# Loading q and k over the hardware DMA queue and running a whole batch of attention ahead of the MoE, in a fused attention and MoE kernel

## The chip, the cores and the metric

The kernel runs on one core of a Trainium2 chip. The metric is the device time of one execution in microseconds (us). All times are medians; each run of a changed kernel stood beside runs of the kernel before on the same chip. A ratio below is the mean time of one kernel's fast runs over the mean time of the other's fast runs of the same rounds, so it is not quite the ratio of the medians quoted beside it.

The *time* is what is measured from outside; the *span* is what the profile covers, and it was about 2 us shorter in nearly every run (415.06 against 412.9 in the profiled run of the changed kernel).

## The reference, cut to what matters

```python
# q, k, v: (8 batches, 8 heads, 576 tokens, 64), f: (8, 8, 576), all fp32
scores = q @ k^T / sqrt(64)
cum    = cumsum(log(clip(f, 1e-4, 1)))             # a forget gate: decay between tokens
scores = where(causal, -1e9, scores + cum_i - cum_j)
x      = softmax(scores) @ v                       # (8, 8, 576, 64)
x      = x.transpose(0, 2, 1, 3).reshape(4608, 512)
h      = x @ w_in                                  # 512 -> 2048
out    = (h * sigmoid(h)) @ w_out                  # 2048 -> 512
```

## The kernel before

Attention goes in 16 steps `n`, each one half batch (four heads). A step has four chunks of scores. A chunk is a matmul into PSUM (`sc`), an exponential on ScalarE into `u`, and a causal mask on VectorE, in place:

```python
sc = patt.tile([P, QH, 512], FP32, name="sc", tag="att")   # 4 PSUM banks, one buffer
...                                                        # matmuls with lhsT = k, rhs = q
nc.scalar.activation(out=u[:, :, c*CW:(c+1)*CW], in_=sc[:, :, 0:CW], func=ACT.Exp, scale=scale)
...
nc.vector.tensor_tensor(out=x, in0=x, in1=mask_broadcast, op=ALU.mult)     # masks(n, c)
```

Then `products` multiplies `u` by the weighted values (`vp`) and by weights alone (`w_bf`, for the sums), into a tile `ps` that takes the same four banks. From it ScalarE copies the sums out, VectorE takes their reciprocals (a quarter at a time, between the chunks of the next step) and writes the normed result to `xT`, the input of the MoE.

The MoE is cut into units of four 128x512 matmuls: `hp` for the first layer, `po` for the second. `fill(n)` puts up to n units between the chunks, so that TensorE has work while ScalarE forms exponentials. Which kind a unit is follows from what is allowed:

```python
def fill(n):
    for _ in range(n):
        a, c = done["m1"], done["m2"]
        can1 = a < 16 * ready["g"] and a < 16 * (c // 16) + 32
        can2 = c < 16 * (a // 16)
        if not can1 and not can2:
            return False                     # nothing left: the gap stays empty
        if can1 and (not can2 or a - c <= 16 + (c % 2)):
            m1_chunk(...)                    # hp, then tanh (th) and gate (gt)
        else:
            m2_part(...)                     # po; after four of them osb and the store
...
for n in range(16):
    scores(n, 0); masks(n, 0); reciprocals(n - 1, 0); fill(3)
    scores(n, 1); masks(n, 1); reciprocals(n - 1, 1); load_qk(n + 2); fill(3)
    scores(n, 2); masks(n, 2); transposes(n + 1, 1); reciprocals(n - 1, 2); fill(3)
    scores(n, 3); transposes(n + 1, 0); masks(n, 3); reciprocals(n - 1, 3); fill(3)
    products([(n, None), (n - 1, 0), (n - 1, 1)]); finished(n - 1)
    fill(4)
```

(The special cases of steps 0 to 2 are cut.) `finished` releases a group of 512 tokens, 32 units, once its tokens are there, which in the steady part is about once in two steps. q and k come by transfers on GpSimd's queue that convert them to bf16 on the way, in runs of one token (64 fp32 values, 256 bytes); VectorE transposes them in blocks of 32x32.

The softmax here doesn't subtract the row's maximum and nothing guards it: scores larger than these inputs give would overflow.

## Time and profile before

The kernel took 394.63 us (394.57 to 395.19 in three runs). The profiled run took 396.2 us with a span of 394.2.

| | before |
|---|---|
| TensorE busy | 85% of the span |
| first MoE product that needs new activations of group 1 | 100.74 us |
| five periods, one per batch | 199.69 us, 39.94 each |
| the rest | 93.77 us |
| transfers on GpSimd's queue and SP's queue, share of 16 engines | 42.6% and 20.8% |
| packets, of them under 512 B | 122871, 114064 |

The three stretches of the table add up to the span: in the steady part a *period* is the time from one group's first product on new activations to the next group's. The prediction below shows the lines that this is read from. In the view of VectorE's costliest groups of the kernel before, the columns after the bar are busy us, mean ns of one, and the idle time before them:

```profile
L185 DVE STREAM_TRANSPOSE qkT<-raw 128x1152 bf16<-128x1152 bf16 x32 | 43.4, 1358 | 0.1
L233 DVE TENSOR_TENSOR u<-u,mask 128x512 bf16<-128x512 bf16 x64 | 27.1, 423 | 57.1 <-ACT u L221 56.7
```

### The profile page before, as it was taken

The numbers are of one execution on the slowest core, as the hardware profiler recorded it, in microseconds if no ns is written. First come the engines' busy times: TensorE is split into PE (matmuls) and PEld (weight loads), VectorE is DVE, ScalarE is ACT, GpSimd is POOL, SyncE is SP. The second block draws the span as 40 slices with busy tenths as digits, with TensorE's granted clock in tenths as the row PEclk, the third lists the DMA queues.
The fourth block names the chain that finished last, engine by engine and source line by source line (L and its number), as shares of the span: only waits on it lengthen the run. The fifth ranks groups of instructions, "written<-read, shape, count | busy, mean of one in ns | idle before, by whom it ended". The sixth has DMA issues, their size and how long they took to land.

```text
span 394.2 us, 9014 instructions
## 1 busy us (share of the span) xinstructions
PE 335.3 (85%) x3853; PEld 161.5 (41%) x3853; DVE 247.6 (63%) x359; ACT 209.0 (53%) x264; POOL 131.0 (33%) x185
## 2 busy tenths in 40 slices
PE   0245499985899989998999899989998998999996
PEld 0123244444344534443444344444444454444442
DVE  3654568836695669665966596659665984644400
ACT  4354367543683568365936583559354923534421
POOL 8397674890905090509150815050000000000000
PEclk9999799996999999999999999999999999999999
DMA  9999999999629654974596469700010000000112
GB/s 165 178 177 150 146 180 172 101 141 171 44 17 136 132 56 29 110 153 53 36 108 156 49 40 95 169 28 0 29 54 29 2 28 28 22 33 27 53 55 80
DMA packets 122871, 33.82 MB, mean 86 GB/s; under 512 B 114064, under 2 KB 118160, under 8 KB 122832
## 3 DMA queue, kind: packets, MB, share of 16 engines
q0 software_dynamic: 75328, 13.05, 42.6%
q1 hardware_dynamic: 45136, 19.62, 20.8%
q10 hardware_dynamic: 2368, 0.59, 0.7%
q8 instruction: 30, 0.49, 0.5%
q14 instruction: 9, 0.07, 0.1%
HBM read 36.85 MB, written 9.44 MB: 117 GB/s over the span
## 4 chain that ended last, share of the span: by engine, by line
PE 61%; DMA 15%; DVE 10%; POOL 6%; ACT 4%; issue 3%; SPq 0%; DVEq 0%; POOLq 0%; ACTq 0%
PE po L327 29%; PE hp L300 21%; PE ps L259 7%; DMA raw<-in_q_dram 4%; DVE qkT L185 4%; PE sc L213 4%; DMA w_out_bf<-in_moe_w_out_dram 3%; DMA vf<-in_v_dram 3%; POOL raw L73 3%; DVE xT L277 3%; POOL vp L175 2%; DMA w_in_bf<-in_moe_w_in_dram 2%; DVE gt L309 2%; DMA raw<-in_k_dram 2%; ACT u L221 2%
## 5 line engine op out<-in xcount | busy, mean ns | idle before, releaser
L300 PE MATMUL hp<-xT,w_in_bf 128*128 128x512 bf16 x576 | 135.0, 380 | 15.4 <-DVE xT L277 11.8
L327 PE MATMUL po<-w_out_bf,gt 128*128 128x512 bf16 x576 | 131.8, 380 | 0.0
L221 ACT ACTIVATE u<-sc 128x1600 bf16<-128x1600 f32 x64 | 96.0, 1500 | 38.8 <-PE sc L213 38.8
L309 DVE SCALAR_TENSOR_TENSOR gt<-th,hp 128x512 bf16<-128x512 bf16 x144 | 92.4, 673 | 38.2 <-ACT th L308 38.1
L308 ACT ACTIVATE th<-hp 128x512 bf16<-128x512 f32 x144 | 83.8, 601 | 59.4 <-PE hp L300 58.5
L300 PEld LDWEIGHTS <-w_in_bf 128*128 128x128 bf16 x576 | 53.4, 98 | 83.1 <-issue 23.2
L327 PEld LDWEIGHTS <-gt 128*128 128x128 bf16 x576 | 53.8, 98 | 65.6 <-issue 3.1
L286 DVE RECIPROCAL rec<-rec 128x144 f32<-128x144 f32 x64 | 65.3, 1031 | 1.6 <-ACT rec L275 1.6
L175 POOL TENSOR_TENSOR vp<-vf,w_bf 128x512 bf16<-128x512 f32 (+1 forms) x40 | 41.2, 1049 | 74.8 <-PE ps L259 67.2
L233 DVE TENSOR_TENSOR u<-u,mask 128x512 bf16<-128x512 bf16 x64 | 27.1, 423 | 57.1 <-ACT u L221 56.7
L213 PE MATMUL sc<-qkT 32*128 32x224 bf16 (+5 forms) x1024 | 36.4, 263 | 22.9 <-ACT u L221 14.6
L73 POOL DMA_DIRECT2D raw<-in_k_dram x60 | 39.8, 671 | 43.1 <-DVE qkT L185 29.4
L336 ACT ACTIVATE osb<-po 128x512 f32<-128x512 f32 x36 | 21.5, 596 | 45.1 <-PE po L327 45.1
L185 DVE STREAM_TRANSPOSE qkT<-raw 128x1152 bf16<-128x1152 bf16 x32 | 43.4, 1358 | 0.1
L73 POOL DMA_DIRECT2D raw<-in_q_dram x60 | 39.3, 663 | 11.6 <-DMA w_out_bf<-in_moe_w_out_dram 4.9
L213 PEld LDWEIGHTS <-qkT 32*128 32x128 bf16 x1024 | 20.4, 97 | 48.3 <-issue 42.7
L277 DVE TENSOR_TENSOR xT<-ps,rec 128x576 bf16<-128x576 f32 x32 | 22.7, 751 | 24.9 <-ACT rec L275 18.0
L259 PE MATMUL ps<-u,vp 128*32 128x128 bf16 (+7 forms) x1096 | 28.9, 265 | 1.6 <-ACT u L221 1.6
L275 ACT ACTIVATE rec<-ps 128x576 f32<-128x576 f32 x16 | 10.4, 650 | 34.5 <-PE ps L259 34.5
L259 PEld LDWEIGHTS <-vp 128*32 128x32 bf16 x1096 | 22.6, 106 | 6.0 <-issue 3.2
L259 PE MATMUL ps<-u,w_bf 128*32 128x64 bf16 (+4 forms) x576 | 18.1, 261 | 6.8 <-ACT u L221 4.8
L259 PEld LDWEIGHTS <-w_bf 128*32 128x32 bf16 x576 | 11.9, 102 | 17.1 <-issue 11.6
(28 smaller groups left out, 25.6 us busy)
## 6 DMA issues: line engine op xcount, KB each, us to landing
out_dram<-osb SPq DMA_DIRECT2D x36, 256.0 KB, 2.1
vf<-in_v_dram SPq DMA_DIRECT2D x32, 256.0 KB, 5.2
raw<-in_k_dram POOLq DMA_DIRECT2D x60, 72.0 KB, 3.5
raw<-in_q_dram POOLq DMA_DIRECT2D x60, 72.0 KB, 3.3
w_in_bf<-in_moe_w_in_dram POOLq DMA_DIRECT2D x8, 256.0 KB, 6.6
w_out_bf<-in_moe_w_out_dram POOLq DMA_DIRECT2D x4, 512.0 KB, 11.4
vf<-in_v_dram SPq DMA_DIRECT2D x8, 128.0 KB, 4.7
first<-in_k_dram ACTq DMA_DIRECT2D x2, 144.0 KB, 3.5
```

The source lines that it names most:

```text
L73: nc.gpsimd.dma_start(out=t[j * T : (j + 1) * T, i, :].rearrange("p (g d) -> p g d", d=D), in_=src[b, QH * g + j, :, :].rearrange("(g t) d ...
L175: nc.gpsimd.tensor_tensor(out=vp[r, c, :, :, :], in0=vst[b][c][r, :, :].rearrange("p h (r x) -> p h x r", x=2), in1=w_bf[r, c, b * H : (b ...
L185: nc.vector.transpose(out=qkT[n][:, i, :, :].rearrange("p x (g t) -> p g x t", t=T), in_=raw[n][:, i, :].rearrange("p (g x e) -> p g x e", ...
L213: nc.tensor.matmul(sc[:, j, lo - c * CW : hi - c * CW], lhsT=t[r, 1, x, k_off(kb) : k_off(kb) + P], rhs=t[r, 0, x, q0 : q0 + hi - lo], sta ...
L221: nc.scalar.activation(out=u[:, :, c * CW : (c + 1) * CW], in_=sc[:, :, 0:CW], func=ACT.Exp, scale=scale)
L259: nc.tensor.matmul(ps[32 * j : 32 * j + 32, base + q0 : base + q1], lhsT=w, rhs=us[n][:, j, o + q0 : o + q1], start=(kb == 0), stop=(kb == ...
L277: nc.vector.tensor_tensor(out=xT[:, 2 * g + h, b * S : (b + 1) * S], in0=src, in1=recs[n][:, :], op=ALU.mult,)
L286: nc.vector.reciprocal(out=recs[n][:, r], in_=recs[n][:, r])
L300: nc.tensor.matmul(hp[:, :], lhsT=w_in_bf[:, cc, fc * P : (fc + 1) * P], rhs=xT[:, cc, t0 : t0 + TG], start=(cc == 0), stop=(cc == NCC - 1),)
L308: nc.scalar.activation(out=th[:, :], in_=hp[:, :], func=ACT.Tanh, scale=0.5)
L309: nc.vector.scalar_tensor_tensor(out=gt[:, fc, :], in0=th[:, :], scalar=1.0, in1=hp[:, :], op0=ALU.add, op1=ALU.mult,)
L327: nc.tensor.matmul(po[:, :], lhsT=gt[:, fc, tb * P : (tb + 1) * P], rhs=w_out_bf[:, fc, :], start=(fc == 0), stop=(fc == NFC - 1),)
```

## The change

The intent was to feed TensorE in the first 50 us, where it is half idle. q and k are loaded by SP's hardware queue in runs of two tokens (512 bytes), with no conversion; GpSimd casts them. The transposes write the natural token order back. Both steps of batch 0 run before any MoE unit, with two four-bank score buffers in PSUM; the second one is given back before the MoE takes its four banks. And the order of filler in the loop is new.

```diff
-    G = S // T
+    G = S // (2 * T)
-    qkp = ... tc.tile_pool(name="qkp", bufs=3)
+    qkp = ... tc.tile_pool(name="qkp", bufs=2)
+    pfirst = tc.tile_pool(name="pfirst", bufs=1, space=PSUM)    # second score buffer, start only
+    att = [patt, pfirst]                                        # taken in turn
...
-                nc.gpsimd.dma_start(out=t[...bf16...], in_=src[...].rearrange("(g t) d -> t g d", t=T))
+            engs[j % len(engs)].dma_start(out=stg[n][...fp32...],
+                in_=src[...].rearrange("(g t c) d -> t g (c d)", t=T, c=2))
+    def cast_qk(n, i):
+        nc.gpsimd.tensor_copy(out=raw[n][:, i, :], in_=stg[n][:, i, :])
...
-            out=qkT[n][:, i, :, :].rearrange("p x (g t) -> p g x t", t=T),
+            out=qkT[n][:, i, :, :].rearrange("p x (g t c) -> p g c x t", t=T, c=2),
...
-            if can1 and (not can2 or a - c <= 16 + (c % 2)):
+            if can1 and not (can2 and (x < fresh or a - c > 16 + (c % 2))):
...
+    # scores, masks and products of steps 0 and 1, then:
+    pfirst_pool.__exit__(None, None, None)
+    pbig = ... tc.tile_pool(name="pbig", bufs=4, space=PSUM)
+    fill(6)
+    transposes(2, 1); transposes(2, 0)
-    for n in range(NQ):
+    for n in range(2, NQ):
...                                          # casts of step n + 1 in the first two gaps
-        fill(3)
+        fill(4)
         products([(n, None), (n - 1, 0), (n - 1, 1)])
-        fill(4)
+        fill(5, 3)                           # the first three of second-layer kind
```

(The loads of weights and values move with it.) So an odd step asks for 3+3+3+4+5 = 18 units in place of 16, out of the same 32 per two steps.

## The prediction

> **What bounds the kernel now.** Words first. The kernel has 16 attention steps n (8 batches, two groups of four heads each); each has four chunks of scores on TensorE (sc), an exponential on ScalarE (u), a mask on VectorE, then products (ps) that end in xT. The MoE is cut into 288 units of four 128x512 matmuls (hp: first layer, po: second) that are put between the chunks as filler. Group g of the MoE needs the attention of whole batches, so two steps release about 32 units.
>
> I read the page's busy line and slices first, then TensorE's costliest group, then busy time by stretch, then the chain of waits, then the timeline of TensorE where it idles. Columns of a timeline: start and length in us, engine, line, operation, tiles, shapes, count, and in brackets the idle time before with what ended it.
>
> ```profile
> PE 335.3 (85%) x3853; PEld 161.5 (41%) x3853; DVE 247.6 (63%) x359; ACT 209.0 (53%) x264; POOL 131.0 (33%) x185
> PE   0245499985899989998999899989998998999996
> L300 PE MATMUL hp<-xT,w_in_bf 128*128 128x512 bf16 x576 | 135.0, 380 | 15.4 <-DVE xT L277 11.8
> ```
>
> TensorE is the bound, except in the first eighth, and its longest waits are for VectorE's xT, not for a DMA. By stretch (length, TensorE busy, weight load, VectorE, ScalarE, Pool, clock, DMA):
>
> ```profile
> 14.40:50.20 35.80, 16.74 (x365) 11.25 (x365) 18.27 (x26) 16.33 (x12) 26.94 (x36) 0.91 1.30 159
> 50.20:100.70 50.50, 42.40 (x546) 20.94 (x543) 34.73 (x49) 27.63 (x33) 31.91 (x43) 0.93 1.29 147
> 140.70:180.60 39.90, 37.28 (x464) 17.55 (x464) 28.75 (x42) 23.97 (x30) 15.46 (x22) 1.00 0.70 87
> 330.10:394.20 64.10, 60.16 (x278) 27.10 (x277) 22.01 (x33) 25.07 (x42) 0.00 (x0) 1.00 0.11 41
> ```
>
> So there are four parts: a start of 50 us with TensorE half idle; 50 to 100.7; five equal periods of 39.94 us, one per batch, from the first real hp of a group (100.74) to that of step 14 (300.43); and 93.8 us of rest. A period has 2.64 us of TensorE idle, three waits that the timeline gives: 1.70 for xT in the even step, 0.73 for gt and 0.21 for a mask in the odd one. This is the end of an even step with filler before the products:
>
> ```profile
> 212.92 0.53 PE L213 MATMUL sc<-qkT 32*128 32x144 bf16 x24
> 213.38 2.76 PE L327 MATMUL po<-w_out_bf,gt 128*128 128x512 bf16 x12
> 216.07 0.87 PE L259 MATMUL ps<-u,w_bf 128*32 128x512 bf16 x36
> 218.26 0.60 PE L300 MATMUL hp<-xT,w_in_bf 128*128 128x512 bf16 x2
> 220.56 3.18 PE L300 MATMUL hp<-xT,w_in_bf 128*128 128x512 bf16 x14 [1.70 <-DVE xT L277]
> ```
>
> And step 4, the only one in steady use that had run out of units before its products:
>
> ```profile
> 91.19 0.53 PE L213 MATMUL sc<-qkT 32*128 32x144 bf16 x24 [1.60 <-ACT u L221]
> 93.33 1.31 PE L259 MATMUL ps<-u,w_bf 128*32 128x512 bf16 x24 [1.61 <-ACT u L221]
> 95.42 0.44 PE L259 MATMUL ps<-u,w_bf 128*32 128x128 bf16 x12 [0.77 <-DVE u L233]
> 95.64 2.88 PE L259 MATMUL ps<-u,vp 128*32 128x448 bf16 x68
> ```
>
> The reader should see that without filler the products wait for the last exponential (1.61) and then the last mask (0.77): 2.4 us that three units hide at 213.38.
>
> [...] the 68 value products above took 2.88 us after the idle stretch and 1.55 at 216.77. [...] steady TensorE waits for no DMA here. [...] a mask that started at 77.47, while the chain of waits has Pool at work on vp until 78.10, took 0.91 us where this mask takes 0.38 elsewhere (215.69). [...] the new transposes write every second bf16, one per 4-byte word. No run yet shows what that costs a transpose (1.36 us now).
>
> **The change part by part.**
> *Loads.* q and k leave Pool's queue (120 issues of 0.67 us, 79 us of Pool) for the SP queue; the packets double. Pool gets 32 casts of 128x1152; I estimate 1.2 to 1.7 us each from its 1.04 us for a two-input 128x512, so some 45 us in all, and Pool, at 15.5 us of a 40 us period, stays idle. Transposes: same count and elements, I take 1.36 us. Gain in the steady part: none, as nothing on TensorE waits there for a load.
>
> *Start.* The instruction order shows both steps of batch 0, then 6 units, then step 2. f still sets VectorE free at 9.5 us. Transposes of k and q, 2 x 1.37: scores at 12.4 (14.43 before). With two score buffers the exponentials run end to end: 13.25 + 4 x 1.53 = 19.4, where a chunk took 2.46. Then exp(1,0) to 20.9, products and the copy (0.65) to 21.7, exps 1 to 3 at 1.5 each to 26.4, mask to 27.2, the rest of the products (0.4 + 2.9, slow clock) to 30.5, copy 31.2, xT 32.7, four reciprocals 36.5, xT 37.9: first hp at **37.9** instead of 51.77. But step 2's first two chunks had been done by then, and are still to come now.
>
> *After it.* Six units, [...] end at 44.9. Step 2's transposes stand behind the sixth gt (46.3) on VectorE: 2 x 1.36, so scores wait until 49.0, some 4 us idle[...]. Step 2: four chunks with three units at 3.15 (163.53 to 166.68), a 13th unit, products 0.9, gt wait 0.7, four units 3.5: 69.5. Step 3: the order puts nine po units, and then none: 3 x 3.15 + 0.5, wait 2.4, products 2.4: 84.3. Step 4 has no unit at all (64 score matmuls in a row): copy and xT 2.1 before its buffer is free, then from the 83.72 to 100.74 that it took before I take off 1.0 for less filler, so **102** in place of 100.74 for the first real hp of group 1. The 14 us won are eaten: the MoE has only the 32 units of group 0 until batch 1 is done, wherever they are put. Estimate for this point: 98 to 105.
>
> *Period.* Units released stay 32, but a full odd step now asks for 18 (po moved ahead), so 14 are left for the even one: the order reads sc24, ps104, hp20, no filler before the products. Even step: wait 2.4 (1.6 + 0.77, as step 4 showed), and still 1.7 for xT, since hp comes right behind. Odd step: 0.73 for gt stays, 0.21 goes. Sum 4.86 against 2.64: +2.2, period 42.2, five of them **+11**.
>
> *Rest.* Same units; fill ahead of the last hp hides its xT wait (0.99). 93.8 - 1 = 92.8.
>
> Sum: 102 + 5 x 42.2 + 92.8 = 405.8 of span, 0.4 more as time: 406. The middle of my range for the start (101) gives **405**.
>
> **The rivals.** (1) *The start's gain holds* (14 us at the first hp, or at least 5): it would if the units' supply did not matter. For: TensorE is half idle there. Against: step 4 starved before already with one filler more. With T = 95 and the waits of the even step half hidden, 391 to 396. (2) *The casts or strided transposes make VectorE the bound.* VectorE works 28.75 of 40 us, but sits right before the products in each step: at 2.0 us a transpose (+0.65), each step's tail would grow by 1.3, 2.6 a period, and the time would be near 418. [...] (3) *DMA*: the q1 queue's 20.8% of 16 engines over 45136 packets is 29 ns a packet; q and k of four steps and two v are 18432 packets, 33 us of all 16 engines, and w_in and w_out some 10 us each (the chain has 9.25 and 12.61 for the last of each): about 55 us, an estimate, and the first po is due at 61. If late, +3 to +6. For: share 1.29 until 100 before. [...]
>
> **Range and chances.** The period's two waits are read from the same instructions (step 4), so +8 to +12 is firm if the order is followed; the start is good to 3.5 us either way; rival 2 has perhaps one chance in six. So 405, 397 to 415. 2% slower begins at 402.5: 0.62; within 2%: 0.33; faster than 386.7 needs rival 1 in full: 0.05.
>
> **What would show it.** First hp near 38, idle TensorE near 45 to 49, group 1's first real hp near 102 (before 100.74), step 4 without filler; periods of 42 us, with two waits in the even step, of 2.4 ahead of ps for u and the mask and of 1.7 ahead of hp for xT; transposes of 1.36; casts under 1.7; DMA share about half in the steady part. I am wrong if the period stays at 40 (waits hidden by something I did not see), if transposes take 2 us or more, or if group 1 starts by 95.

Its sum came to 405.8 us of span, put down as 405 us of time. Two stood in the sum of the start: a slow stretch within the six units (their 7.0 us, 37.9 to 44.9, still hold it) and about 1.7 us for a second one in step 2, so the terms printed for step 2 fall short of its 69.5 by about that much. The slow clock that it reckons with for the value products of step 1 (2.9 us) is what step 4 showed: 2.88 us, with a granted clock of 0.50 from 91.8 to 98.6 us. The DMA share of about half was the estimate; no trace showed it before the change.

## The result and the profile after

The changed kernel took 415.56 us (414.1 to 416.6, four runs) against 394.91 us beside it (394.57 to 395.57): ratio 1.0518, 95% interval 1.0481 to 1.0556. That is slower, as expected, but just above the range of 397 to 415.

The page's busy line, its slices and TensorE's costliest group, after:

```profile
PE 343.9 (83%) x3853; PEld 166.8 (40%) x3853; DVE 257.4 (62%) x357; ACT 208.8 (51%) x264; POOL 89.3 (22%) x97
PE   0475699836899789987999699969996999999996
PEclk9998889985999989999999899989999999999999
L306 PE MATMUL hp<-xT,w_in_bf 128*128 128x512 bf16 x576 | 138.2, 389 | 19.1 <-DVE xT L283 14.6
```

The second digit of the PE row is now 4 where it was 2: the start does run earlier. But a 3 and several 6s have come in between 20% and 75% of the span, and the clock's row (9 is full speed) has a 5 at the end of the start and single 8s in the loop. TensorE has the same 3853 instructions and 8.6 us more of busy time: some of them ran slower.

By stretch (length, TensorE busy, weight load, VectorE, ScalarE, GpSimd, clock, share of the DMA engines, GB/s), after:

```profile
39.20:105.10 65.90, 48.13 (x567) 23.17 (x568) 38.28 (x51) 30.85 (x35) 21.31 (x20) 0.83 0.89 173
105.10:148.80 43.70, 38.73 (x464) 18.69 (x464) 29.83 (x42) 23.97 (x30) 9.66 (x10) 0.96 0.39 91
148.80:190.90 42.10, 37.26 (x464) 17.72 (x464) 29.49 (x42) 23.97 (x30) 9.26 (x10) 1.00 0.49 105
```

The first real product of group 1 stands at 105.06 us, later than before the change, although the first MoE product moved to 39.16. Then come periods of 43.74, 42.11, 43.82, 43.76 and 41.91 us. The two shown hold the same 464 matmuls; the first took 1.47 us more of TensorE's time, at clock 0.96.

TensorE's timeline where an even step of the changed kernel ends (start, length, engine, line, operation, tiles, shapes, count, idle time before):

```profile
139.51 0.53 PE L219 MATMUL sc<-qkT 32*128 32x144 bf16 x24
141.71 0.76 PE L265 MATMUL ps<-u,w_bf 128*32 128x512 bf16 x24 [1.67 <-ACT u L227]
143.48 0.44 PE L265 MATMUL ps<-u,w_bf 128*32 128x128 bf16 x12 [1.02 <-DVE u L239]
143.71 2.88 PE L265 MATMUL ps<-u,vp 128*32 128x448 bf16 x68
146.52 0.79 PE L306 MATMUL hp<-xT,w_in_bf 128*128 128x512 bf16 x2
148.80 1.46 PE L306 MATMUL hp<-xT,w_in_bf 128*128 128x512 bf16 x6 [1.49 <-DVE xT L283]
```

Compare it with the same place in the prediction (from 212.92): no filler between the last scores and the products, so TensorE waits 1.67 us for the exponential, then 1.02 for a mask; then the 68 value products take 2.88 us instead of 1.55; then it waits for xT as before. The starving was predicted, but the second wait is longer here than the 0.77 allowed for (over the five periods it is 0.39 to 1.02), and the slow products are a cost that the sum did not have in the steady part.

VectorE's groups after, to be set beside the two lines shown of before:

```profile
L191 DVE STREAM_TRANSPOSE qkT<-raw 128x1152 bf16<-128x1152 bf16 x32 | 46.0, 1445 | 0.0
L239 DVE TENSOR_TENSOR u<-u,mask 128x512 bf16<-128x512 bf16 x64 | 33.5, 527 | 63.0 <-ACT u L227 62.8
```

The transposes cost 6% more, the masks 25% more on average, though the masks did not change. None of TensorE's waits in the view of waits is for a transfer, before or after; the two queues' share of the DMA engines fell from 63.4% to 47.3%, and packets under 512 B from 114064 to 40336.

| span by part, us | before | after | difference |
|---|---|---|---|
| to the first real product of group 1 | 100.74 | 105.06 | +4.3 |
| five periods | 199.69 | 215.34 | +15.7 |
| the rest | 93.77 | 92.50 | -1.3 |
| span | 394.2 | 412.9 | +18.7 |

### The profile page after: what moved, and what is told of

It reads as the page before. It is cut to its first block, busy times and chain, and to the rows that moved or that the text cites. A ratio compares the mean times of both kernels' runs of the same rounds, so it can differ in the third digit from the quotient of the medians.

```text
span 412.9 us, 9054 instructions
## 1 busy us (share of the span) xinstructions
PE 343.9 (83%) x3853; PEld 166.8 (40%) x3853; DVE 257.4 (62%) x357; ACT 208.8 (51%) x264; POOL 89.3 (22%) x97
## 4 chain that ended last, share of the span: by engine, by line
PE 61%; DVE 27%; ACT 8%; issue 1%; DMA 1%; ACTq 0%; DVEq 0%
PE po L333 26%; PE hp L306 22%; DVE qkT L191 9%; PE ps L265 9%; DVE rec L292 6%; ACT u L227 6%; DVE u L239 5%; PE sc L219 4%; DVE gt L315 4%; DVE xT L283 3%; ACT rec L281 1%; ACT th L314 1%; DMA f_sb<-in_f_dram 1%; DVE cum L154 0%; PE wps L170 0%
## 5 line engine op out<-in xcount | busy, mean ns | idle before, releaser
L306 PE MATMUL hp<-xT,w_in_bf 128*128 128x512 bf16 x576 | 138.2, 389 | 19.1 <-DVE xT L283 14.6
L315 DVE SCALAR_TENSOR_TENSOR gt<-th,hp 128x512 bf16<-128x512 bf16 x144 | 93.2, 672 | 40.0 <-ACT th L314 40.0
L306 PEld LDWEIGHTS <-w_in_bf 128*128 128x128 bf16 x576 | 54.4, 99 | 90.4 <-issue 32.8
L239 DVE TENSOR_TENSOR u<-u,mask 128x512 bf16<-128x512 bf16 x64 | 33.5, 527 | 63.0 <-ACT u L227 62.8
L89 POOL CAST raw<-stg 128x1152 bf16<-128x1152 f32 x32 | 36.7, 1150 | 166.4 <-DMA stg<-in_k_dram 131.8
L191 DVE STREAM_TRANSPOSE qkT<-raw 128x1152 bf16<-128x1152 bf16 x32 | 46.0, 1445 | 0.0
L265 PE MATMUL ps<-u,w_bf 128*32 128x64 bf16 (+4 forms) x576 | 18.8, 263 | 19.1 <-ACT u L227 10.8
L265 PE MATMUL ps<-u,vp 128*32 128x128 bf16 (+7 forms) x1096 | 32.4, 286 | 0.0
L265 PEld LDWEIGHTS <-vp 128*32 128x32 bf16 x1096 | 25.2, 114 | 5.1 <-issue 1.8
```

The source lines that it names most:

```text
L89: nc.gpsimd.tensor_copy(out=raw[n][:, i, :], in_=stg[n][:, i, :])
L191: nc.vector.transpose(out=qkT[n][:, i, :, :].rearrange("p x (g t c) -> p g c x t", t=T, c=2), in_=raw[n][:, i, :].rearrange("p (g c x e) - ...
L239: nc.vector.tensor_tensor(out=x, in0=x, in1=m[:, None, :].to_broadcast([P, QH, w]), op=ALU.mult)
L265: nc.tensor.matmul(ps[32 * j : 32 * j + 32, base + q0 : base + q1], lhsT=w, rhs=us[n][:, j, o + q0 : o + q1], start=(kb == 0), stop=(kb == ...
L306: nc.tensor.matmul(hp[:, :], lhsT=w_in_bf[:, cc, fc * P : (fc + 1) * P], rhs=xT[:, cc, t0 : t0 + TG], start=(cc == 0), stop=(cc == NCC - 1),)
L315: nc.vector.scalar_tensor_tensor(out=gt[:, fc, :], in0=th[:, :], scalar=1.0, in1=hp[:, :], op0=ALU.add, op1=ALU.mult,)
```

## The experiments

Twelve kernels were run, all correct, each timed over three rounds. They are told in the order of the argument. Spans are split as above: T is the end of the start, then five periods, then the rest (92.5 to 93.2 in all versions with the new order, 93.7 with the old).

| run | time, us | ratio (95%) | T | five periods |
|---|---|---|---|---|
| after | 415.56 | 1.0518 (1.0481 to 1.0556) | 105.06 | 215.34 |
| e3_order_only | 409.77 | 1.0363 (1.0345 to 1.0382) | 106.22 | 208.92 |
| e2_loads_only | 403.74 (three fast runs) | 1.0246 (1.0190 to 1.0302) | slow run | slow run |
| e12_loads_4out | 398.42 | 1.0090 (1.0061 to 1.0120) | 100.89 | 201.89 |
| e1_fill_before | 407.30 | 1.0306 (1.0249 to 1.0363) | 106.19 | 204.42 |
| e11_fill_before_4out | 401.37 | 1.0141 (1.0109 to 1.0172) | 103.44 | 201.08 |
| e8_mask_first | 407.15 | 1.0297 (1.0279 to 1.0314) | 103.78 | 208.83 |
| e9_cast_twice | 425.24 | 1.0774 (1.0750 to 1.0798) | 106.58 | 221.83 |
| e7_dummy_mm | 413.36 | 1.0447 (1.0417 to 1.0478) | 105.79 | 213.01 |
| e10_one_buffer | 420.63 | 1.0628 (1.0576 to 1.0679) | 109.99 | 215.24 |
| e6_plan | 376.32 | 0.9527 (0.9494 to 0.9559) | 88.01 | 193.91 |
| e13_plan_old_loads | 381.03 | 0.9631 (0.9595 to 0.9668) | 94.49 | 190.95 |
| e14_plan_tuned | 372.83 | 0.9426 (0.9403 to 0.9448) | 89.59 | 188.59 |

The ratios are to the kernel before, whose median beside them was 394.91 to 395.40 us. T and the periods come from one profiled run each. In the last three kernels no wait marks the first product on new activations, so T there is the first MoE product of group 1, about 0.5 us earlier than the mark used for the others (in e13, 94.49 against 94.93).

### The new order with the old loads

```diff
 # the changed kernel, with load_qk, first load and transposes of the kernel before, and no cast_qk
-            nc.gpsimd.tensor_copy(out=raw[n][:, i, :], in_=stg[n][:, i, :])
+            nc.gpsimd.dma_start(...)          # q and k converted on the way
```

> The order, PSUM use and filler of the changed kernel with the loads of the kernel before (256-byte runs converted by Pool's own queue, no casts, plain transposes). Theory: the loss stays, less what casts add to the mask wait; periods 41.5 to 43 as the clock falls; 407 to 415. Rival 1 (casts and transposes): 395 to 400. A third way: Pool's queue is slow to bring step 1's q and k, so the start is 3 to 5 us later.

Measured: 409.77 us, 14.6 over the kernel before. The end of an even step in this run:

```profile
142.80 0.76 PE L266 MATMUL ps<-u,w_bf 128*32 128x512 bf16 x24 [1.67 <-ACT u L228]
143.81 0.41 PE L266 MATMUL ps<-u,w_bf 128*32 128x128 bf16 x12 [0.25 <-DVE u L240]
144.03 1.56 PE L266 MATMUL ps<-u,vp 128*32 128x448 bf16 x68
```

The wait for the exponential is the same 1.67 us, so it belongs to the order. The wait for the mask is 0.25 in every period, against 0.39 to 1.02 after the change, and the value products are slow once in five periods (2.5 us) in place of three times. The five periods are 6.4 us shorter than after the change. Of these, 2.5 are mask waits (5 x 0.25 against 3.72 in all), 2.9 are value products (8.74 against 11.68) and 0.7 are waits for gates. So the order costs most of the loss, and something in the loads adds 5.8 us (415.56 - 409.77) on top of it.

### The new loads with the old order

```diff
 # the kernel before, with load_qk, cast_qk and transposes of the change
```

> The order, PSUM use and filler of the kernel before, with the new loads alone (512-byte runs on the SP queue, casts on Pool, transposes that write every second element). Theory: transposes cost 0.08 us more each and a mask is now and then held by a cast for up to 0.7 us, mostly behind filler: periods 40 to 40.4, start a little earlier, so 392 to 397. Rival 1 (loads and casts make the loss): at least half of the 20 us shows here, 405 or more.

Measured: 403.74 us in the median of the three fast runs (403.25, 403.74, 407.69), between the two expectations. The profiled run was slow (413.07), so its waits are only named here: it too had ScalarE waiting for the store of an output tile. The next pair of runs shows that with fast profiles.

### The old filler counts in the new order, and the output buffers

```diff
-        fill(4)                      # after the last scores
+        fill(3)
         products(...)
-            fill(5, 3)
+            fill(4)
```

> The changed kernel with the filler counts of the kernel before in the main loop (3, 3, 3, 3 before the products, 4 after them), so that three po units stand ahead of the products of every even step. Theory (empty filler, then a slow clock): the wait of 2.1 to 2.7 us ahead of the even products goes, and with it the half-clock value products, so the five periods fall from 43.1 to about 40.2 us: 14 us, 401 to 402. Rival 1 (the casts on Pool and the strided transposes make the loss): periods stay near 43, time 413 or more. Rival 2 (only the waits count, the clock was slow for another reason): 2.2 a period, 404 to 405.

Measured: 407.30 us, above the 401 to 402 and the 404 to 405 that were expected, and below the 413 of rival 1. The wait of 1.67 us and the slow products are gone from all periods, which shows what caused them. But less than half of the loss came back (8.3 us), since the wait for xT grew from 1.7 to as much as 3.44 us. The timeline of SP's queue and then of ScalarE and TensorE in this run tells why:

```profile
130.38 1.91 SPq L81 DMA_DIRECT2D stg<-in_k_dram  x4
132.33 1.95 SPq L81 DMA_DIRECT2D stg<-in_q_dram  x4
134.38 5.63 SPq L97 DMA_DIRECT2D vf<-in_v_dram  x5
140.10 5.50 SPq L343 DMA_DIRECT2D out_dram<-osb  x3
```

```profile
144.64 0.60 ACT L342 ACTIVATE osb<-po 128x512 f32<-128x512 f32 x1 [3.92 <-DMA out_dram<-osb]
145.14 0.64 ACT L281 ACTIVATE rec<-ps 128x576 f32<-128x576 f32 x1
145.81 1.42 DVE L283 TENSOR_TENSOR xT<-ps,rec 128x576 bf16<-128x576 f32 x2 [2.73 <-ACT rec L281]
147.29 1.02 PE L306 MATMUL hp<-xT,w_in_bf 128*128 128x512 bf16 x4 [2.72 <-DVE xT L283]
```

Thirteen loads take SP 9.7 us to issue, and the stores stand behind them. With two output buffers, ScalarE can't copy the next output tile out until a store has landed (3.92 us), and the copy that leads to xT is next in its line. (The changed kernel itself has no wait of ScalarE for a store in its view of waits; the stall came up with the old counts.) The test is two more buffers, in this order and in the old one:

```diff
-    opool = ... tc.tile_pool(name="opool", bufs=2)
+    opool = ... tc.tile_pool(name="opool", bufs=4)
```

> The changed kernel with the filler counts of the kernel before in the main loop, and four output buffers in place of two. Theory A (with those counts only the wait of the copy to the output for the output's transfer, up to 4.6 us, behind thirteen loads on one queue, was left): that wait is gone, the wait for the transposed activations falls from 1.7 to 3.4 us to 0.7 to 1.0, the five periods are 39.8 to 40.3 us as before the change, and the time is 400 to 403 us. Theory B (the wait for activations has another source, the casts or the slow clock): periods stay near 40.9 and the time at 405 to 408.

> The kernel before with only the new loads, casts and transposes, and four output buffers so that no copy to the output waits behind loads. Theory A (beside the output stall the new loads cost next to nothing, and the order is what costs): periods of 39.9 to 40.6 us and 394 to 398 us. Theory B (casts and transposes slow VectorE and with it the whole loop): periods of 41 us or more and 400 us or more.

Measured: 401.37 and 398.42 us. Neither has a wait of ScalarE for a store, and the wait for xT is back at 1.70, not down to the 0.7 to 1.0 that e11 expected. Both sets of periods are near those of before: 40.05 to 40.43 and 40.06 to 40.61, each against 39.94. The end of an even step in the first of the two:

```profile
136.57 2.54 PE L333 MATMUL po<-w_out_bf,gt 128*128 128x512 bf16 x11 [0.16 <-issue]
139.03 0.87 PE L265 MATMUL ps<-u,w_bf 128*32 128x512 bf16 x36
139.73 1.55 PE L265 MATMUL ps<-u,vp 128*32 128x448 bf16 x68
141.44 0.38 PE L306 MATMUL hp<-xT,w_in_bf 128*128 128x512 bf16 x1 [0.16 <-issue]
143.52 0.81 PE L306 MATMUL hp<-xT,w_in_bf 128*128 128x512 bf16 x3 [1.70 <-DVE xT L283]
```

So 14.2 of the 20.65 us lost come back by filler counts and output buffers alone. The new loads in the old order, without the stall, cost 3.0 us (398.42 against 395.40). e12 ended 0.4 above its first expectation (394 to 398), and its mean mask took 493 ns where 423 was usual.

### What the casts do

GpSimd's casts take 1.15 us each and delay masks. In the timeline of the changed kernel, GpSimd and VectorE:

```profile
138.01 1.15 POOL L89 CAST raw<-stg 128x1152 bf16<-128x1152 f32 x1 [28.38 <-DMA stg<-in_k_dram]
```

```profile
138.47 0.97 DVE L239 TENSOR_TENSOR u<-u,mask 128x512 bf16<-128x512 bf16 x1 [1.76 <-ACT u L227]
139.36 1.46 DVE L191 STREAM_TRANSPOSE qkT<-raw 128x1152 bf16<-128x1152 bf16 x1
140.73 0.99 DVE L292 RECIPROCAL rec<-rec 128x144 f32<-128x144 f32 x1
141.65 1.42 DVE L191 STREAM_TRANSPOSE qkT<-raw 128x1152 bf16<-128x1152 bf16 x1
142.98 0.44 DVE L239 TENSOR_TENSOR u<-u,mask 128x512 bf16<-128x512 bf16 x1
```

The mask of 138.47 ends just after the cast does (139.44 against 139.16), and takes 0.97 us where the one at 142.98 takes 0.44. All after it on VectorE is later by half a microsecond, and at the end of that line stands the mask which TensorE waited 1.02 us for. The transposes in that line, 0.09 us longer each than before, have a smaller part in it: in the fifth period, where the last cast had ended at 285.1 us, the wait for the mask was 0.39 us, against 0.25 in e3 (neither casts nor these transposes) and 0.68 to 1.02 in the four periods with casts. Two runs test it: all casts from step 4 on twice, and the last mask ahead of the second transpose.

```diff
-        nc.gpsimd.tensor_copy(out=raw[n][:, i, :], in_=stg[n][:, i, :])
+        for _ in range(2 if n > 3 else 1):
+            nc.gpsimd.tensor_copy(out=raw[n][:, i, :], in_=stg[n][:, i, :])
```

> The changed kernel with every q and k cast of the steps from 4 on done twice on GpSimd, which has the time. Theory A (a Pool cast holds VectorE's mask products while it runs, and a mask that is held comes late to the value products): the mean mask product rises from 527 to 560 ns or more, the waits for masks in odd steps are longer or more frequent, and the time rises by 1 to 6 us, to 416 to 422. Theory B (the casts are harmless beside VectorE, the mask waits come from the order alone): masks stay at 530 ns and the time at 415 us, within 1.

Measured: 425.24 us, 9.7 more than the changed kernel for 24 more casts on an engine that is 22% busy. That is beyond the 1 to 6 us expected. The mean mask went to 589 ns, and the periods grew to 45.11, 44.38, 45.47, 44.76 and 42.11 us; the last one hardly changed (41.91 in the changed kernel), and in it no cast runs beside the masks of the even step: all casts are over by 294.4 us. Nor did the transposes wait for the doubled casts: VectorE has no wait for GpSimd in that run's view of waits.

```diff
         scores(n, 3)
-        if more:
-            transposes(n + 1, 0)
         masks(n, 3)
+        if more:
+            transposes(n + 1, 0)
```

> The changed kernel with the last mask of a step ahead of the second transpose on VectorE. The wait ahead of the even products then ends with the exponential: 1.67 us instead of 1.67 + 0.4 to 1.0. Theory: 0.4 to 1.0 a period from the wait and, if it is the length of the wait that costs the clock, 1.3 in three of five periods: periods 41.4 and all with value products of 1.56 us, 406 to 408. Rival 2 (the clock does not hang on this wait): only the 0.7 a period, so 411 to 413. It may cost up to 0.3 a step elsewhere as the transpose comes later.

Measured: 407.15 us, 8.4 less than the changed kernel, by moving one line. The wait for the mask is gone in four of five periods:

```profile
140.43 0.88 PE L265 MATMUL ps<-u,w_bf 128*32 128x512 bf16 x36 [1.67 <-ACT u L227]
141.12 1.56 PE L265 MATMUL ps<-u,vp 128*32 128x448 bf16 x68
```

The masks did not become shorter (564 ns on average, against 474 in e3, which has no casts). They still are held by casts; they only no longer stand last in VectorE's line before the products. In the one period left, at 222.78 us, the mask wait of 0.77 us stayed and the value products were slow (2.48 us). The five periods, 208.83 us, are as long as those of e3 (208.92), which has no casts at all. So what the loads added to the periods is matched by this delay and what follows from it. The match is in part chance, as the moved line also takes away the 0.25 us of mask wait that e3 has without any cast.

### The slow products

The value products took about 2.9 us in some periods and 1.56 in others. In the slow ones of the changed kernel the granted clock was 0.50. No single idle stretch of the steady part of the changed kernel is longer than 1.7 us. To tell the gap from other causes, six matmuls that nobody reads went into it:

```diff
+            if n % 2 == 0:
+                dummies(6)          # 128x512, into a tile of the MoE's banks, not read
             products([(n, None), (n - 1, 0), (n - 1, 1)])
```

> The changed kernel with six more 128x512 matmuls, into a bank that nobody reads, put where TensorE waits 1.67 us for the probabilities of an even step. They wait for nothing, so TensorE is busy in that gap. Theory A (the half-clock value products come of the idle TensorE before them): every group's value products take 1.5 to 1.6 us as in the warm groups of the changed kernel, none 2.8; the five periods are 41.5 to 42.5 us; the time is 4 to 6 us under that of the changed kernel, 409 to 412 us. Theory B [...]: products of 2.5 to 2.9 us stay in three groups of five and the time is 415 us or more. If the six matmuls (1.3 us) delay the products, periods grow by up to that at most where the wait was shorter than they are.

```profile
140.93 1.24 PE L348 MATMUL hp<-xT,w_in_bf 128*128 128x512 bf16 x5 [0.16 <-issue]
142.44 0.76 PE L265 MATMUL ps<-u,w_bf 128*32 128x512 bf16 x24 [0.27 <-DVE rec L292]
144.71 0.42 PE L265 MATMUL ps<-u,w_bf 128*32 128x128 bf16 x12 [1.52 <-DVE u L239]
144.94 1.56 PE L265 MATMUL ps<-u,vp 128*32 128x448 bf16 x68
```

Measured: 413.36 us. The products took 1.56 us in all five periods, even behind a mask wait of 1.52 us. The same holds for all 30 even-step products of the six other fast profiles that have units in this gap (e1, e11, e12, e6, e13, e14), so the long idle gap before them is the cause. The gain was 2.2 us rather than 4 to 6: the products won 3.9 us over the five periods, the waits for masks grew by 0.9 and those for xT by 0.4. The periods, 41.80 to 43.00 us, are longer than the 41.5 to 42.5 expected in three of five. Useless work is a probe here; useful work in that gap (e11) is worth far more.

Why does the same gap cost the clock in one period and not in the next? The clock record of the traces answers part of it. In the traces of the kernels before and after, any two changes of the granted clock lie a whole multiple of 3.41 us apart: in the changed kernel the stretches at half clock lasted 6.83, 3.41, 13.65 and three times 3.41 us, and those at full clock between them 6.83, 34.13, 40.96, 81.92 and 40.96 us. So these traces show a grid of windows, and it does not follow the kernel's steps. These are windows of the changed kernel (length, TensorE busy, clock, share of the DMA engines, GB/s):

```profile
140.11:143.52 3.41, 0.80 (x28) 1.00 1.04 193
143.52:146.94 3.42, 3.42 (x82) 0.50 0.99 269
184.48:187.90 3.42, 1.77 (x76) 1.00 1.37 222
187.90:191.31 3.41, 1.71 (x44) 1.00 1.12 294
```

At 140 us both waits fall into one window, TensorE is busy for 0.80 us of it, and the next window runs at half clock. At 184 us the waits fall across two windows with 1.77 and 1.71 us of work, and the clock stays full. The other two slow windows follow 1.63 and 0.84 us of work, and the last fast period has 1.96 and 1.74. Where a gap falls on the grid changes from period to period; e3 has the same gap five times (1.67 + 0.25) and slow products once. Busy time of the window alone does not tell all: the window from 95.74 us, with 1.80 us of work at half clock, was followed by half clock again, and in e1 a wait of 3.44 us for xT was followed by products at full speed (14 of 128x512 in 3.18 us).

### What the eight banks bought

```diff
-    att = [patt, pfirst]
+    att = [patt]
```

> The changed kernel with one four-bank score buffer at the start in place of two; all else as it is. Theory A (the two buffers let scores be formed while ScalarE still reads the ones before, and this is what brought the first MoE product and the batch's attention forward): the first MoE product, at 39.2 us in the changed kernel, comes at 41 to 44 us, and the first product of group 1 (105.1) 2 to 4 us later; the time is 417 to 420 us. Theory B (the start is bound by the loads and by VectorE, so the second buffer brings nothing): first MoE product within 1 us of 39.2 and the time within 1.5 us of 415.6.

Measured: 420.63 us, with the first MoE product at 43.08 and T at 109.99, against 39.16 and 105.06. T comes 4.9 us later, where 2 to 4 were expected. The second score buffer is worth 4 to 5 us, and it is not what made the kernel slower. The time is 0.6 above the top of what was expected.

### A version that deals the filler out by hand

The changed kernel starts early and then starves in three places: 4 us before step 2's scores, the end of step 3 with all of step 4, and the end of every even step. The next version keeps the change's loads and banks, and gives each gap its units in a table; step 2's transposes and first two chunks go ahead of the MoE, the four output buffers of e11 are kept.

```diff
+    PLAN = {2: ['', '', '111', '1111', '11'], 3: ['11', '11', '11', '122', '22'],
+            4: ['22', '22', '22', '222', '22211'],
+            5: ['111', '111', '111', '111', '1122'], 6: ['222', '222', '222', '222', '2211'], ...}
+    # 1: an hp unit, 2: a po unit; five gaps per step, the last one behind the products
-        fill(3)
+        run(n, 0)
```

> A candidate that keeps the change's loads, casts and banks: four output buffers, scores of step 2 formed ahead of the first MoE unit, and matmul units dealt to every gap between value products, with two output products kept for the wait on the transposed activations. Theory A (the even steps lack filler only by how it is dealt): no wait over 0.5 us at an even step's products, the first MoE product of group 1 by 85 to 92 us, periods of 38.3 to 39.6 us, time 372 to 386 us. Theory B (some engine other than TensorE binds below 40 us per group, VectorE or ScalarE): periods stay at 39.5 or more with new waits for that engine, time 386 to 396 us; or the weights of the MoE arrive too late for the earlier start and the first group's gain is lost.

Measured: 376.32 us, ratio 0.9527. T is 88.01, and the periods are 38.2 to 39.1. No product of an even step waits more than 0.5 us in the steady part, and the two po units behind the products cover the wait for xT. The next run takes the same plan with the old loads:

```diff
 # e6 with load_qk, first load and transposes of the kernel before, no casts
```

> The version with the dealt filler (376.3 us) with the loads of the kernel before: q and k converted on the way by GpSimd's transfers, no casts. Theory A (the win of that version is the order and the filler, the new loads add little to it): 374 to 381 us. Theory B (the early order needs the faster loads of the change): the first MoE product comes 3 us or more later than 40.3 us and the time is 382 to 390 us.

Measured: 381.03 us, between the two expectations. The first MoE product comes at 48.82, 8.5 us later, for TensorE waits 10.8 us before step 2's scores; by group 1, T is 6.5 later. VectorE has nothing to transpose until k of step 2 has landed, and the product xT that frees the score buffer stands behind these transposes in its line:

```profile
38.37 1.38 DVE L192 STREAM_TRANSPOSE qkT<-raw 128x1152 bf16<-128x1152 bf16 x1 [9.83 <-DMA raw<-in_k_dram]
43.05 0.85 PE L220 MATMUL sc<-qkT 32*128 32x400 bf16 x8 [10.78 <-DVE xT L284]
```

After that each period is 0.6 us shorter than with casts (38.19 against 38.78 on average). So in this order the new loads pay at the start and cost a little in the loop. One rival stays untested: on GpSimd's queue these loads were issued behind those of `w_in`, and a version that issues them first was not run.

The last version takes what e6's trace still showed: 0.80 us for a gate in each odd step, 0.28 to 0.43 for masks, and 2.9 once at step 3.

```diff
-        reciprocals(n - 1, 2); run(n, 2); scores(n, 3); transposes(n + 1, 0); masks(n, 3)
+        run(n, 2); reciprocals(n - 1, 2); scores(n, 3); masks(n, 3); transposes(n + 1, 0)
-    3: [..., '122', '22'], 4: [..., '22211']
+    3: [..., '122222', ''], 4: [..., '2211']
```

> The version with the dealt filler, tuned by its trace: the masks of the last score chunk ahead of the second transpose, the third reciprocal behind the matmul units of its gap, and the two units that stood behind the products of step 3 ahead of them. Theory A (these were VectorE's place in line, not its load): the waits of 0.80 us for the gates and of 0.28 to 0.43 us for the masks are gone, the one of 2.9 us at step 3 falls to 1 us or less, periods of 38.0 to 38.4 us, time 367 to 372 us. Theory B (VectorE only moves the wait elsewhere): periods stay at 38.9 us and the time at 374 to 378 us.

Measured: 372.83 us, ratio 0.9426, in no doubt against both kernels. The same place in an even step:

```profile
158.07 0.53 PE L219 MATMUL sc<-qkT 32*128 32x144 bf16 x24
158.53 2.76 PE L333 MATMUL po<-w_out_bf,gt 128*128 128x512 bf16 x12
161.22 0.87 PE L265 MATMUL ps<-u,w_bf 128*32 128x512 bf16 x36
161.92 1.55 PE L265 MATMUL ps<-u,vp 128*32 128x448 bf16 x68
163.41 1.90 PE L333 MATMUL po<-w_out_bf,gt 128*128 128x512 bf16 x8
165.14 2.03 PE L306 MATMUL hp<-xT,w_in_bf 128*128 128x512 bf16 x8
```

There is no wait in it. Periods are 37.5 to 38.1 us (38.0 to 38.4 expected). The waits for masks are gone; of those for gates 0.4 us at most is left. The time missed its expectation (367 to 372) by 0.8 because the start got worse, not better: with the units of step 3 drawn forward, TensorE waits 4.8 us there for a gate and 2.2 for a buffer, so T is 89.59 in place of 88.01. All of the gain over e6 is in the periods.

## Why the prediction was right or wrong

**Right: the direction and the waits.** It said that odd steps would eat the units of even ones, that the products of an even step would wait for the exponential and then a mask, and that the start's 14 us would be lost by group 1. The trace shows each of these, and e1 and e11 show the first as the cause of most of the loss. The order alone (e3) gave periods of 41.58 to 42.51 us where 42.2 was predicted. The rest was predicted at 92.8 and took 92.5. TensorE waited for no transfer.

**Wrong: the size, by 10.6 us (415.56 against 405).** Split by the prediction's own terms:

| term | predicted | measured | miss |
|---|---|---|---|
| first real product of group 1 | 101 | 105.06 | +4.1 |
| five periods | 5 x 42.2 = 211 | 215.34 | +4.3 |
| rest | 92.8 | 92.5 | -0.3 |
| span to time | 0.4 | 2.1 | +1.7 |

These add up to 9.8 us for the profiled run, which took 415.06. From its last sum (405.2) to the 405 put down, and from that run to the median of four, come the other 0.7.

- *Loads: "Gain in the steady part: none".* This step failed by leaving out a loss. The casts took 1.15 us, where 1.2 to 1.7 was estimated, on an engine that is mostly idle, and the prediction even showed a mask that took 0.91 us in place of 0.38 while GpSimd worked on `vp`; then it put the price at zero. The loads cost 5.8 us in the new order (e3 against after), and doubling the casts cost 9.7 more (e9). The transposes, which rival 2 feared at 2.0 us, took 1.445 rather than 1.36: VectorE did not become the bound, at 30 of 43 us. The masks' place in its line was what counted (e8).
- *Period: "Sum 4.86 against 2.64: +2.2".* (Its own terms add up to 4.83.) What failed is that the sum counts waits alone and takes TensorE's busy time as unchanged. The waits were right: 4.65 to 5.17 us in a period against 4.86. Busy time was 37.3 us in two periods, as before, but 38.7 to 38.8 in the three with half-clock products, which makes 4.2 of the 4.3 us missed (e7 removes it). The prediction had noted 2.88 against 1.55 us for the value products behind an idle stretch, and did not carry it into the period. That the waits came out right is in part luck: the 0.77 for the mask was read at a step without casts, the new order alone gives 0.25 (e3), and the mean of 0.74 after the change is made up by the new loads. So the order alone stayed 2.1 us under the 211 predicted, and the loads added 6.4.
- *The clock: 2.88 us "after the idle stretch".* The trace has the granted clock at 0.50 there, but the idle stretch was one of several waits: before the slow products of step 4 no single wait was longer than 1.61 us.
- *Start: 102, taken down to 101 for the middle of a range.* Each step was late by a little: first product 39.16 (37.9), scores of step 2 at 51.22 (49.0), step 3 at 71.34 (69.5), its products' end at 86.2 (84.3). By step 2 it was 2.2 us behind, 1.3 of it there at the first MoE product and 1 more because the six units took 8.0 us and not 7.0: the clock was at half (0.50) for their first 5.4 us (to 44.54), longer than the sum had allowed. Step 4 added another 1.1. How much of this is the chip's clock, which was 0.83 in this stretch, and how much the order was not separated; T varied from 103.4 to 106.6 among the versions that share the start's order and its two buffers.
- *"0.4 more as time".* 394.2 was the span of a run that took 396.2, and it was compared with the median of other runs, 394.63. Span and time must be of one run.
- *"The 14 us won are eaten ... wherever they are put".* As a limit this was false. e6 has the same 32 units and the same release rule, and starts group 1 at 88.01. What ate the gain was idle TensorE in steps 2 to 4, and that could be scheduled away. Rival 1 was right that the start could pay, only not in this order.

What stays open: the miss of the start between clock and order, as said; how little work in a window brings the half clock (in the changed kernel a window with 1.63 us did, and one with 1.71 did not); and how the old loads of e13 would do in another place of their queue.

## What to carry to other kernels

Filler work is a budget: a change that gives one gap more units takes them from another, so count units released against units asked for in every gap, and put them where the longest wait ends. A gap can cost more than its own length: three of the five here, of 2.4 to 2.7 us, slowed the products behind them by 1.2 to 1.3 us. A free engine is not a free operation: a cast of 1.15 us on an idle engine cost time because it held instructions of another engine (a mask took 0.97 us rather than 0.44), one of which stood last in line before the bound one, and moving that instruction one place forward won 8.4 us back. When loads move onto a queue that also carries stores, see how long the stores wait behind them (here thirteen loads took 9.7 us to issue, and ScalarE waited up to 4.6 us for a store in e1), and give the stores' buffers that much slack (with four in place of two, e11 had no such wait).
